# Narrower scores and shared-out probability blocks in the first batches, and permuted weight columns, in a fused attention and gated feed-forward kernel

## The chip, the cores and the metric

The kernel runs on one core of a Trainium2 chip. The metric is the device time of one execution in microseconds (us), the median of several runs. Inside the core, TensorE (PE in the profile) multiplies matrices, VectorE (DVE), ScalarE (ACT) and GpSimd (POOL) do the element work, and the queue of SyncE (SP) issues the transfers between device memory and the on-chip memory. PEld is the part of TensorE that loads the stationary operand of a multiplication. The engines run side by side, each through its own list of instructions in a fixed order, and wait for one another by semaphores.

## What is computed

Attention over 8 batches, 8 heads, 576 positions, 64 features for each head, and then two matrix products with a gate between them, over the 4608 rows that the attention gives.

```python
scores = q @ k.T / 8            # (8, 8, 576, 576)
rel = pos[:, None] - pos[None, :]
mask_local   = (rel >= 0) & (rel < 32)                      # heads 0 to 3
mask_strided = (rel >= 0) & (pos % 32 equal on both sides)  # heads 4 to 7
attn = softmax(where(mask, scores, -1e9)) @ v
x = attn as (4608, 512)
h = x @ w_in                    # (4608, 2048)
out = (h * clip(h + 3, 0, 6) / 6) @ w_out                   # (4608, 512)
```

So few scores count: a local head needs a band of 32 positions, a strided head 18 positions for each of the 32 residues.

## The kernel before

**The feed-forward part** carries nearly all of the multiplying. Every operand is held as a high and a low part, and a product is three matmuls (high by high, high by low, low by high), each 128 by 128 by 512 columns. Batches 0, 1 and 2 are done one by one in `ffn`: for each of 16 chunks `fc`, four first products over the four head pairs `c` (lines 848 to 850), a gate (ACT line 769, DVE line 772), a split of the gated tile into `gh` (ACT line 783) and `gl` (POOL line 787), and four second products into the accumulators `acc` (lines 825 to 827). Batches 3 to 7 and the leftover rows are done two at a time with a scheme that needs seven products for eight (Strassen's): `super_tile` and `fast_tile`, whose first products are lines 1121 to 1123 (tiles `P`) and whose second products in `fast_tile` are lines 1444 to 1446 (tiles `cP`). The last take the weights as the stationary operand and pick every second column of them, `d::2`, so that a later transpose on DVE gives rows of the output.

**The weights** are loaded once, in 32 parts of 128 by 512, during the first batch. `weight_part` sends each through a chain: two ACT passes (lines 281 and 285), a join on DVE (line 289), a rounded copy `hi` on ACT or POOL (lines 295 and 297), and the difference `lo` on POOL (line 301). The tiles are `rawi`/`rawo`, `fi`/`fo`, `wi`/`wo`.

**The attention** is done in pairs of heads (`pair`; c = 0 and 1 are local, 2 and 3 strided). For each pair and each of its two heads j: scores on PE into `ps`, a masked copy into the tile `e`, a maximum (DVE, line 637), its subtraction (POOL, line 641), the exponential (ACT, line 645), a sum and its inverse (DVE, lines 651 and 654), the scaling (POOL, line 658). Then the 32 by 32 blocks of `e` are transposed and set out into the mostly zero tiles `atloc` or `atstr`, and PE multiplies these with the values into `pv`. Two forms of these steps matter here.

- Scores of strided pairs are `wide` (64 rows by 36 columns, line 593) in every batch but 1: fewer matmuls, but half of the result is unused, so four ACT copies of 32 partitions (line 619) pick the rest out and a POOL instruction adds the mask (line 633). The narrow form (line 601) takes twice the matmuls and one DVE instruction (line 626) does copy and mask together.
- Blocks are set out by DVE in batches 0 and 1: a transpose for each block, 4 for a strided head (line 677), 6 for a local head (line 680). From batch 2 on one DVE transpose turns all blocks in place (line 683), and ACT copies them out (lines 690 and 693). The two local pairs of batch 0 do it by PE instead.

Finally `keep_x` takes `pv` into the operand of the first product, in two or three pieces: a rounded copy (ACT, line 419) and, in batches 0 and 1, the low part (DVE, line 422). The pieces of a pair share one key, so that copy, difference, copy, difference follow each other.

**The order of the work** is made when the program is built. Every step is handed to `Plan.op` with the engine or engines that may do it, a cost, what it reads and writes and a due time; `Plan.emit` sorts them into one list for each engine by a list schedule over these costs. Where it sees PE idle in the first 100 us it puts in matmuls on an identity tile (`idle`, line 1562) that feed nothing. `T0` is the planned time of the first batch's products, from which the other due times follow. No engine leaves its list's order at run time.

Of the kernel before, what the change touches and what calls it, by code (L numbers as in the profile page):

```python
# [29 lines left out]
TOK = 512  # L30
TURNS = ((0, 2, 1, 3), (2, 0, 3, 1)) + ((0, 2, 1, 3),) * 6
AHEAD = 27.0
OPEN = 6.0
HIENG = {"ACT": 0.63, "POOL": 0.7}

T0 = 44.0
TILE = 98.5
SUPER = 182.0  # L40
SECOND = 142.0
# [132 lines left out]
def attention_ffn(ctx: ExitStack, tc, q, k, v, w_in, w_out, out):  # L174
# [85 lines left out]
    def weight_part(k, w, g, i):  # L260
        key = wkey(w, g, i)
        fc = FQ * g if w == "i" else FQ * g + i + 1
        due = T0 + fc * TILE / NFC - 5.0 + 0.01 * k
        fkey = ("x", 1, 1 - (k // 2 % 2 if k < 20 else 0), k % 2)
        name = f"{w}{g}{i}"

        def load():
            if w == "i":
                src = w_in[i * P:(i + 1) * P, g * TOK:(g + 1) * TOK]
            else:  # L270
                src = w_out[(g * FQ + i) * P:(g * FQ + i + 1) * P, :]
            raw = new(wp, key, [P, TOK, 2], I32, f"raw{name}")
            nc.sync.dma_start(raw, src.bitcast(I32).rearrange("p (n t) -> p n t", t=2))

        def bits():
            raw = tiles[key]
            return raw.rearrange("p n t -> p (n t)")[:, :TOK]

        def high():
            f = new(xp, fkey, [P, TOK], I32, f"f{name}")  # L280
            nc.scalar.activation(f.bitcast(F32), tiles[key][:, :, 1].bitcast(F32), AF.Prelu, scale=2.0 ** -112, alpha=2.0 ** 32)

        def low():
            raw = tiles[key].bitcast(U16).rearrange("p n (t u) -> p n t u", u=2)[:, :, 0, 1]
            nc.scalar.activation(bits(), raw, AF.Copy, scale=2.0 ** -13, bias=2.0 ** -14 - 0.5)

        def join():
            f = tiles[fkey]
            nc.vector.scalar_tensor_tensor(out=f, in0=f, scalar=3, in1=bits(),  # L289
                                           op0=ALU.logical_shift_left, op1=ALU.bitwise_or)  # L290

        def hi(e):
            t = new(wp, key, [P, 2, TOK], F32R, f"w{name}")
            if e == "ACT":
                nc.scalar.copy(t[:, 0], tiles[fkey].bitcast(F32))
            else:
                nc.gpsimd.tensor_copy(t[:, 0], tiles[fkey].bitcast(F32))

        def lo():
            t = tiles[key]  # L300
            nc.gpsimd.tensor_tensor(out=t[:, 1], in0=tiles[fkey].bitcast(F32), in1=t[:, 0].bitcast(F32), op=ALU.subtract)  # L301
# [21 lines left out]
    def either(us):  # L323
        return {"POOL": us, "DVE": us}

    def zero(key, pool, shape, dtype, us, due, name):

        def go(e):
            on(e).memset(new(pool, key, shape, dtype, name), 0.0)
            if key[0] == "e":  # L330
                t = tiles[key]
                on(e).memset(t[:, :NQB * WIN].rearrange("p (u x) -> p u x", x=WIN)[:, :, 2 * PAD:], 1.0e-9)
                on(e).memset(t[:, NQB * WIN:NQB * WIN + 8 * PAD].rearrange("p (u x) -> p u x", x=PAD)[:, :, NPOS:NPOS + 1], 1.0e-9)
        op(either(us), 0, go, writes=[key], due=due)

    def timing(g):
        b = g // NPAIR
# [60 lines left out]
    def x_keys(b, c):  # L398
        return [("x", b, c, i) for i in range(2)] if b < 2 else [raw_key(b, c)]

    def keep_x(nm, b, c, puts, due):

        xk, lk = x_keys(b, c), ("left", c, b)
        strided = c >= NPAIR // 2
        begun = []
        for n, (bkey, what, place, size, rest) in enumerate(puts):
            def to(i, place=place, rest=rest):
                return place(left[c][:, LEFT * b:LEFT * b + LEFT] if rest else tiles[xk[i]])

            def homes():  # L410
                if not begun:
                    begun.append(1)
                    for i, x in enumerate(xk):
                        new(xp, x, [P, TOK], F32R if b < 2 else F32, f"x{nm}{i}")

            def hi(bkey=bkey, what=what, to=to, rest=rest):
                if not rest:
                    homes()
                nc.scalar.copy(to(0), what(tiles[bkey.key]))

            def lo(bkey=bkey, what=what, to=to):
# [4 lines left out]
            op("ACT", 0.15 + size * (0.0019 if strided else 0.00085), hi, reads=[bkey] + (xk if rest else []), writes=kk, give=bkey if last and whole else None, due=due + n)  # L426
            if not whole:
                op("DVE", 0.15 + size * (0.002 if strided else 0.00105), lo, reads=[bkey], writes=kk, give=bkey if last else None, due=due + 0.2 + n)

# [3 lines left out]
    def pair(g):  # L433
# [237 lines left out]
        for j in range(2):  # L671
            def turn(j=j):
                at, e = tiles[akeys[j]], e_whole(j)
                for a in range(n // PAD):
# [3 lines left out]
                        continue  # L678
                    for h in range(2):
                        nc.vector.transpose(at[PAD * (a + h):PAD * (a + h) + PAD, :, rows], e[rows, :, PAD * h:PAD * h + PAD])  # L680
            if b >= 2:
                def flip(j=j):
                    nc.vector.transpose(e_whole(j)[:, :, :2 * PAD if loc else PAD], e_whole(j)[:, :, :2 * PAD if loc else PAD])  # L683

# [10 lines left out]
                def again(j=j):  # L695
                    nc.gpsimd.memset(e_whole(j)[:, :, NPOS:NPOS + 1], 1.0e-9)
# [20 lines left out]
        def values():  # L717
# [12 lines left out]
        op("PE", 1.25 * slow, values, reads=[*akeys, *vkeys], writes=[*vb, *xk, lk], take=vb, due=due - 1001,  # L730
           room=0.0 if early else ROOM, mode="v")
        if first:
            half = S // 2
# [56 lines left out]

    def out_ops(i, uk, name, rows, due, last):
        def ob():
            o = new(xp, uk, [P, DM], F32, f"ob{name}_{i}")
            if last and i % 2:
                nc.vector.tensor_scalar_mul(o, tiles["acc", i], 1.0 / 6.0)
            else:
                nc.scalar.activation(o, tiles["acc", i], AF.Copy, scale=1.0 / 6.0)

        def store():
            o = tiles[uk]  # L800
# [9 lines left out]
    def ffn(b):  # L810
        s0, puts = start[b], []
        chunk = TILE / NFC
        xk = {c: x_keys(b, c) if b < 2 else [("x", 1, c, i) for i in range(2)] for c in range(NCC)}

        def mm2(fc, gk):
            wkeys = [wkey("o", fc // FQ, fc % FQ), wkey("o", fc // FQ, fc % FQ) + ("lo",)]
# [17 lines left out]
        def first_product(fc):  # L834
# [3 lines left out]
            for n_, c in enumerate(TURNS[b]):  # L838
                wkeys = [wkey("i", fc // FQ, c), wkey("i", fc // FQ, c) + ("lo",)]

                def mm1(n_=n_, c=c, wkeys=wkeys):
# [9 lines left out]
                op("PE", 0.683, mm1, reads=xk[c] + wkeys, writes=[pk],  # L851
                   due=s0 + (fc + n_ * 0.12) * chunk, mode="f")
            return fc, pk, uk, gk

# [430 lines left out]
    def fast_tile(si):  # L1285
# [87 lines left out]
        def second_of(s):  # L1373
# [5 lines left out]
            for j, nm in enumerate(SECONDS):  # L1379
# [53 lines left out]
                for d in range(2):  # L1433
                    bank = ("acc", d + 2 * (nm in ("P2", "P5", "P3")))

                    def mm(d=d, bank=bank, gks=gks, wk=wk, fresh=fresh, nm=nm):
# [3 lines left out]
                        w = home(wk).rearrange("p q (h d) -> p q h d", h=2)  # L1440
                        for q in range(2):
                            gh, gl = (half_of(gks[q], x) for x in range(2))
                            wh, wl = (w[:, q, h, d::2] for h in range(2))
                            nc.tensor.matmul(acc, wh, gh, start=fresh and q == 0, stop=False, skip_group_check=not fresh)  # L1444
                            nc.tensor.matmul(acc, wh, gl, start=False, stop=False, skip_group_check=not fresh)  # L1445
                            nc.tensor.matmul(acc, wl, gh, start=False, stop=q == 1, skip_group_check=not fresh)  # L1446
# [62 lines left out]
    def first_tiles():  # L1509
        tiles["qplain"] = ap.tile([P, S + STRIDE * PAD], F32, tag="qq", name="qplain")  # L1510
        tiles["kplain"] = ap.tile([P, PAD + 2 * S], F32, tag="kk", name="kplain")
        nc.gpsimd.memset(tiles["kplain"][:, :PAD], 0.0)
        nc.gpsimd.memset(tiles["qplain"][:, S:].rearrange("c (r m) -> c r m", m=PAD)[:, :, NPOS:], 0.0)
        tiles["at64"] = ap.tile([P, 2, 3 * QB], F32, tag="vt", name="at64")
    op("POOL", 0.1, first_tiles, writes=["plain", ("at64", 0), ("at64", 1)], due=-30)
# [80 lines left out]
```

## Time and profile before

| | |
|---|---|
| median of 3 runs | 875.98 us (873.19 to 877.65) |
| profiled execution | 873.75 us, of which the profile's span is 871.9 us |
| PE busy | 851.9 us, 98% of the span |
| DVE, ACT, POOL busy | 539.3, 557.8, 614.7 us (62, 64, 70%) |
| mean granted TensorE clock | 0.992 |

All rows are of that one profiled execution; the profiled execution is 2.2 us under the median. A busy PE is not always PE at its full pace, since matmuls overlap: the pace is read from the starts of neighbouring matmuls. The rows of a group give the count, the busy time in us and the mean of one in ns; a row of the timeline gives the start and the duration in us and, in brackets, the idle time of the engine before it and what ended it.

### The profile page before, as it was taken

What the parts mean: (1) busy time and instruction counts of PE and PEld (TensorE: products, weight loads), DVE (VectorE), ACT (ScalarE), POOL (GpSimd) and SP (SyncE); (2) the same over time, 40 slices, a digit from 0 to 9 for tenths busy, and PEclk for the clock granted to TensorE, in tenths of its full rate; (3) what the DMA queues carried; (4) which work ended last, traced back from release to release, by engine and by line L of the source; (5) the groups of instructions that cost most, each with busy time, mean ns of one, the idle gap of its engine ahead of it and who ended that gap; (6) DMA issues with size and microseconds to landing.
All of it is one profiled execution on the core that took longest, in us unless ns stands there. A gap on an engine that the chain in (4) does not pass through costs nothing.

```text
span 871.9 us, 18946 instructions
## 1 busy us (share of the span) xinstructions
PE 851.9 (98%) x6962; PEld 687.7 (79%) x6962; DVE 539.3 (62%) x898; ACT 557.8 (64%) x1246; POOL 614.7 (70%) x606
## 2 busy tenths in 40 slices
PE   9889999999999999999999999999999999999996
PEld 6667778878878788888888888788888778888884
DVE  5698877344544548454546672566776987655586
ACT  3697657678778766777668855776645555454441
POOL 4688876688447799756767993666974978667572
PEclk9899999999999999999999999999999999999998
DMA  8968714888974456899999998976566577766536
GB/s 214 322 140 243 220 28 93 236 265 239 299 200 111 112 141 163 233 250 259 259 262 282 300 284 213 253 188 198 181 195 183 178 207 214 231 190 188 178 121 145
DMA packets 323308, 179.12 MB, mean 205 GB/s; under 512 B 182864, under 2 KB 300368, under 8 KB 323216
## 3 DMA queue, kind: packets, MB, share of 16 engines
q1 hardware_dynamic: 318564, 176.27, 71.9%
q10 hardware_dynamic: 4652, 1.64, 0.9%
q8 instruction: 55, 0.90, 0.4%
q14 instruction: 37, 0.30, 0.1%
HBM read 136.97 MB, written 40.89 MB: 204 GB/s over the span
## 4 chain that ended last, share of the span: by engine, by line
PE 87%; DMA 5%; POOL 3%; DVE 2%; issue 1%; ACT 1%; SPq 0%; ACTq 0%; POOLq 0%
PE P L1121 9%; PE P L1123 8%; PE P L1122 8%; PE cP L1444 6%; PE cP L1446 6%; PE cP L1445 6%; PE acc L825 5%; PE ph L848 5%; PE acc L827 5%; PE acc L826 4%; PE ph L850 4%; PE ph L849 4%; PE acc L1206 4%; PE acc L1208 3%; PE acc L1207 3%; PE pv L392 2%
## 5 line engine op out<-in xcount | busy, mean ns | idle before, releaser
L1462 DVE SCALAR_TENSOR_TENSOR C<-cP,C 128x512 f32<-128x512 f32 x96 | 65.7, 688 | 44.9 <-PE cP L1446 44.3
L787 POOL TENSOR_TENSOR gl<-u,gh 128x512 fp32r<-128x512 f32 x48 | 65.2, 1359 | 32.2 <-ACT gh L783 16.0
L1133 DVE TENSOR_TENSOR G<-P,G 128x512 f32<-128x512 f32 x64 | 44.0, 689 | 65.6 <-PE P L1123 52.8
L1121 PE MATMUL P<-B_T,wr 128*128 128x512 f32 x192 | 76.2, 397 | 3.4 <-ACT G L1128 2.3
L825 PE MATMUL acc<-wo,gh 128*128 128x512 f32 x192 | 77.2, 402 | 0.0
L827 PE MATMUL acc<-wo,gl 128*128 128x512 f32 x192 | 75.2, 392 | 0.1
L1123 PE MATMUL P<-B_T,wr 128*128 128x512 f32 x192 | 75.0, 391 | 0.0
L1122 PE MATMUL P<-B_T,wr 128*128 128x512 f32 x192 | 74.9, 390 | 0.0
L826 PE MATMUL acc<-wo,gh 128*128 128x512 f32 x192 | 74.9, 390 | 0.0
L1128 ACT COPY G<-P 128x512 f32<-128x512 f32 x64 | 37.6, 587 | 54.1 <-PE P L1123 53.8
L1359 POOL TENSOR_TENSOR sp<-G,sp 128x512 fp32r<-128x512 f32 x34 | 47.2, 1399 | 25.6 <-ACT sp L1355 23.4
L658 POOL TENSOR_TENSOR e<-e,st 128x144 f32<-128x144 f32 (+1 forms) x64 | 44.6, 700 | 20.2 <-DVE st L654 17.2
L772 DVE SCALAR_TENSOR_TENSOR u<-u,ph 128x512 f32<-128x512 f32 x48 | 32.7, 684 | 37.9 <-ACT u L769 37.8
L848 PE MATMUL ph<-x,wi 128*128 128x512 f32 x128 | 51.9, 406 | 2.0 <-DVE u L772 1.1
L693 ACT COPY atloc<-e 32x192 f32<-32x192 f32 x144 | 50.8, 353 | 2.5 <-DVE e L683 1.1
L849 PE MATMUL ph<-x,wi 128*128 128x512 f32 x128 | 50.1, 391 | 1.1 <-DVE fo L289 0.7
L769 ACT ACTIVATE u<-ph,three 128x512 f32<-128x512 f32 x48 | 33.0, 688 | 27.7 <-PE ph L850 27.3
L850 PE MATMUL ph<-x,wi 128*128 128x512 f32 x128 | 50.2, 392 | 0.5 <-POOL wi L301 0.5
L1121 PE MATMUL P<-B_B,wr 128*128 128x512 f32 x120 | 47.1, 393 | 0.0
L637 DVE TENSOR_REDUCE st<-e 128x8 f32<-128x144 f32 (+1 forms) x64 | 25.6, 413 | 34.5 <-POOL e L633 34.3
L1123 PE MATMUL P<-B_B,wr 128*128 128x512 f32 x120 | 46.8, 390 | 0.0
L1122 PE MATMUL P<-B_B,wr 128*128 128x512 f32 x120 | 46.8, 390 | 0.0
(604 smaller groups left out, 2669.1 us busy)
## 6 DMA issues: line engine op xcount, KB each, us to landing
wr<-dA SPq DMA_DIRECT2D x72, 256.0 KB
or<-do SPq DMA_DIRECT2D x32, 512.0 KB
wr<-dSu SPq DMA_DIRECT2D x48, 256.0 KB
wr<-dSv SPq DMA_DIRECT2D x48, 256.0 KB
or<-do SPq DMA_DIRECT2D x48, 256.0 KB
rawi<-in_moe_w_in_dram SPq DMA_DIRECT2D x16, 512.0 KB
rawo<-in_moe_w_out_dram SPq DMA_DIRECT2D x16, 512.0 KB
do<-wo SPq DMA_DIRECT2D x16, 512.0 KB
```

The lines of the kernel that those rows point to most:

```text
L787: (nc.vector if tail else nc.gpsimd).tensor_tensor(out=to, in0=src(), in1=tiles[gk[0]].bitcast(F32), op=ALU.subtract)
L825: nc.tensor.matmul(acc, gh, woh, start=fc == 0, stop=False)
L826: nc.tensor.matmul(acc, gh, wol, start=False, stop=False)
L827: nc.tensor.matmul(acc, gl, woh, start=False, stop=end)
L848: nc.tensor.matmul(ph, wih, xh, start=n_ == 0, stop=False)
L849: nc.tensor.matmul(ph, wih, xl, start=False, stop=False)
L850: nc.tensor.matmul(ph, wil, xh, start=False, stop=n_ == NCC - 1)
L1121: nc.tensor.matmul(ph, wh, xh, start=fresh and k == 0, stop=False, skip_group_check=not fresh)
L1122: nc.tensor.matmul(ph, wh, xl, start=False, stop=False, skip_group_check=not fresh)
L1123: nc.tensor.matmul(ph, wl, xh, start=False, stop=k == 1, skip_group_check=not fresh)
L1444: nc.tensor.matmul(acc, wh, gh, start=fresh and q == 0, stop=False, skip_group_check=not fresh)
L1462: nc.vector.scalar_tensor_tensor(out=tiles[ck], in0=tiles[bank], scalar=1.0 / 6.0, in1=tiles[ck], op0=ALU.mult, op1=ALU.add)
```

## The change

Three things are changed.

1. **Strided pairs of batch 0** take the narrow scores of batch 1, and the strided pairs of batch 0 and all pairs of batch 1 turn their blocks by one transpose in place. In batches 0 to 4 (`b < FREE`) the copies that set the blocks out are planned one by one, each on ACT, POOL or DVE, where it was DVE alone (batches 0 and 1) or ACT alone (from batch 2).
2. **`keep_x`** has a key for each piece in batches 0 and 1, so that the copy of the second piece no longer waits for the difference of the first; copies of leftover rows get a due time 3 us later. `T0` goes from 44 to 42.
3. **Columns of `w_out`** are stored so that within each half of 256 the even ones stand ahead of the odd ones. The second products of `fast_tile` then read 128 neighbouring columns. The rounded copy and the difference of each `w_out` part read with a step of two, and `out_ops`, which takes `acc` to the output tile `ob`, writes with a step of two.

```diff
-T0 = 44.0
+T0 = 42.0
...
+        def whole():
+            f = tiles[fkey].bitcast(F32)
+            return f if w == "i" else f.rearrange("p (h e d) -> p h d e", h=2, d=2)
+
+        def part(x):
+            t = tiles[key][:, x]
+            return t if w == "i" else t.rearrange("p (h d e) -> p h d e", h=2, d=2)
...
-                nc.gpsimd.tensor_copy(t[:, 0], tiles[fkey].bitcast(F32))
+                nc.gpsimd.tensor_copy(part(0), whole())
...
-            nc.gpsimd.tensor_tensor(out=t[:, 1], in0=tiles[fkey].bitcast(F32), in1=t[:, 0].bitcast(F32), op=ALU.subtract)
+            nc.gpsimd.tensor_tensor(out=part(1), in0=whole(), in1=part(0).bitcast(F32), op=ALU.subtract)
...
-            kk = [lk] if rest else xk
+            kk = [lk] if rest else xk if whole else [("xh", b, c, n)] + ([] if n else xk)
...
-                op("DVE", ..., lo, reads=[bkey], writes=kk, ..., due=due + 0.2 + n)
+                op("DVE", ..., lo, reads=[bkey, ("xh", b, c, n)], writes=[("xl", b, c, n)], ..., due=due + 0.2 + n)
...
-        wide = not loc and b != 1
+        wide = not loc and b > 1
...
-            if b >= 2:
+            if b >= 2 or b == 1 or b == 0 and not loc:
...
-                op("ACT", 6 * 0.31 if loc else 4 * 0.36, spread, reads=[ekeys[j]], writes=[akeys[j]], due=due - 1.9 + j)
+                if b < FREE:
+                    for a in range(n // PAD):
+                        for h in range(1 + loc):
+                            def set_out(e, a=a, h=h, j=j):
...
+                                if e == "ACT":
+                                    nc.scalar.copy(at, x)
+                                else:
+                                    on(e).tensor_copy(at, x)
...
+                            op({"ACT": 0.33, "POOL": 0.42, "DVE": 0.37} if loc else {"ACT": 0.4, "POOL": 0.5, "DVE": 0.44}, 0, set_out,
+                               reads=[ekeys[j], ("zero",) + akeys[j]], writes=own, due=due - 1.9 + j)
+                else:
+                    op("ACT", 6 * 0.31 if loc else 4 * 0.36, spread, reads=[ekeys[j]], writes=[akeys[j]], due=due - 1.9 + j)
...
-            o = new(xp, uk, [P, DM], F32, f"ob{name}_{i}")
+            o = new(xp, uk, [P, DM], F32, f"ob{name}_{i}").rearrange("p (h e d) -> p h d e", h=2, d=2)
+            acc = tiles["acc", i].rearrange("p (h d e) -> p h d e", h=2, d=2)
...
-                            wh, wl = (w[:, q, h, d::2] for h in range(2))
+                            wh, wl = (w[:, q, h, P * d:P * d + P] for h in range(2))
```

Counted over the whole program: DVE loses 56 transposes of single blocks and gains 12 in place and 62 copies; ACT loses 47 copies of blocks, the 16 copies of wide scores and 6 rounded weight copies; POOL gains 41 copies of blocks, 6 rounded weight copies and 8 small fills and loses 4 mask additions. PE gets 64 score matmuls more and 5 identity matmuls less (each of these runs as two passes). The transfers are the same, in nearly the same order.

In what follows the number behind a tile's name tells two tiles apart (`e_130` and `e_228` are the two heads of a pair; `st` holds maxima and sums; `ps_20` is the scores of pair c = 2, head 0; `pe` is the PE's turned block of the local pairs).

On ACT, at the strided pair c = 2 of batch 0 (rows of before, then of the changed kernel), the exponentials of the local pair's two heads stood apart:

```order
L645 ACTIVATE e_130<-e_130 96x6x64
L619 COPY e_130<-ps_20_450 32x8x18 x4
L645 ACTIVATE e_228<-e_228 96x6x64
L619 COPY e_228<-ps_21_451 32x8x18 x4
L506 COPY kt_3_289<-kp_30_530 128x288
```

```order
L654 ACTIVATE e_186<-e_186 96x6x64
L654 ACTIVATE e_233<-e_233 96x6x64
L515 COPY qt_3_289<-qp_30_524 128x288
L515 COPY qt_3_289<-qp_31_525 128x288
L654 ACTIVATE e_186<-e_186 128x8x18
```

The eight copies of wide scores are gone, and the second exponential follows the first.

On DVE, a little later, where the turn of pair 2 and the first steps of the local pair c = 1 meet (before, then changed):

```order
L677 STREAM_TRANSPOSE atstr_269<-e_130 32x8x32 x4
L651 TENSOR_REDUCE st_2_508<-e_228 128x8
L626 TENSOR_TENSOR e_130<-ps_10_599,mband 96x6x64
L628 MEMSET e_130 32x32
L654 RECIPROCAL st_2_508<-st_2_508 128x8
L637 TENSOR_REDUCE st_1_677<-e_130 96x6
L626 TENSOR_TENSOR e_228<-ps_11_600,mband 96x6x64
L628 MEMSET e_228 32x32
L677 STREAM_TRANSPOSE atstr_272<-e_228 32x8x32 x4
L422 TENSOR_TENSOR x_01_703<-pv_00_638,x_00_702 128x288
L651 TENSOR_REDUCE st_1_677<-e_130 96x6
L637 TENSOR_REDUCE st_1_677<-e_228 96x6
```

```order
L692 STREAM_TRANSPOSE e_186<-e_186 128x256
L517 COPY kt_3_290<-kp_31_580 128x288
L660 TENSOR_REDUCE st_2_545<-e_233 128x8
L663 RECIPROCAL st_2_545<-st_2_545 128x8
L692 STREAM_TRANSPOSE e_233<-e_233 128x256
L635 TENSOR_TENSOR e_186<-ps_10_626,mband 96x6x64
L637 MEMSET e_186 32x32
L635 TENSOR_TENSOR e_233<-ps_11_627,mband 96x6x64
L637 MEMSET e_233 32x32
L646 TENSOR_REDUCE st_1_707<-e_186 96x6
L646 TENSOR_REDUCE st_1_707<-e_233 96x6
```

Between the first mask addition of pair 1 and the maximum of its second head there stood a turn of four transposes, a low part and a sum; now the two heads' steps follow each other.

On POOL, around the scaling of pair 3 (before, then changed):

```order
L301 TENSOR_TENSOR wi_840<-fi_727,wi_840 128x512
L1529 MEMSET vloc 32x128
L658 TENSOR_TENSOR e_130<-e_130,st_3_785 128x8x18
L658 TENSOR_TENSOR e_228<-e_228,st_3_785 128x8x18
L301 TENSOR_TENSOR wi_917<-fi_828,wi_917 128x512
L301 TENSOR_TENSOR wo_924<-fo_902,wo_924 128x512
```

```order
L667 TENSOR_TENSOR e_233<-e_233,st_3_841 128x8x18
L718 COPY atstr_270<-e_186 32x8x32 x2
L307 CAST wi_965<-fi_900 128x512
L705 MEMSET e_186 128x8
L718 COPY atstr_273<-e_233 32x8x32
L310 TENSOR_TENSOR wi_948<-fi_858,wi_948 128x512
L705 MEMSET e_233 128x8
L310 TENSOR_TENSOR wi_965<-fi_900,wi_965 128x512
```

Three of the eight block copies of pair 3 stand on POOL, ahead of weight parts.

More of the change, by code (lines that the diff above doesn't have):

```diff
@@ L32 @@
 AHEAD = 27.0
+LEFTS = 3.0
+FREE = 5
 OPEN = 6.0
 HIENG = {"ACT": 0.63, "POOL": 0.7}
-T0 = 44.0
+T0 = 42.0
 TILE = 98.5
@@ L290, in join @@
                                            op0=ALU.logical_shift_left, op1=ALU.bitwise_or)
+        def whole():
[4 more added lines that the diff above has]
+            return t if w == "i" else t.rearrange("p (h d e) -> p h d e", h=2, d=2)
         def hi(e):
-            t = new(wp, key, [P, 2, TOK], F32R, f"w{name}")
+            new(wp, key, [P, 2, TOK], F32R, f"w{name}")
             if e == "ACT":
-                nc.scalar.copy(t[:, 0], tiles[fkey].bitcast(F32))
+                nc.scalar.copy(part(0), whole())
             else:
-                nc.gpsimd.tensor_copy(t[:, 0], tiles[fkey].bitcast(F32))
+                nc.gpsimd.tensor_copy(part(0), whole())
         def lo():
-            t = tiles[key]
-            nc.gpsimd.tensor_tensor(out=t[:, 1], in0=tiles[fkey].bitcast(F32), in1=t[:, 0].bitcast(F32), op=ALU.subtract)
+            nc.gpsimd.tensor_tensor(out=part(1), in0=whole(), in1=part(0).bitcast(F32), op=ALU.subtract)
         op("SP", 0.53, load, writes=[key], due=-49 + 0.01 * k if k < 4 else -48.4 + 0.01 * k if k < 6 else -2 + 0.1 * k if k < 16 else due - 20.0, early=7.0 if k < 16 else due - 30.0, after=1.6 if k < 16 else 1.25)
@@ L333, in go @@
                 on(e).memset(t[:, NQB * WIN:NQB * WIN + 8 * PAD].rearrange("p (u x) -> p u x", x=PAD)[:, :, NPOS:NPOS + 1], 1.0e-9)
-        op(either(us), 0, go, writes=[key], due=due)
+        op(either(us), 0, go, writes=[key, ("zero",) + key], due=due)
     def timing(g):
@@ L422, in lo @@
                 nc.vector.tensor_tensor(out=to(1), in0=what(tiles[bkey.key]), in1=to(0).bitcast(F32), op=ALU.subtract)
-            kk = [lk] if rest else xk
             last = all(x[0] is not bkey for x in puts[n + 1:])
             whole = rest or b >= 2
-            op("ACT", 0.15 + size * (0.0019 if strided else 0.00085), hi, reads=[bkey] + (xk if rest else []), writes=kk, give=bkey if last and whole else None, due=due + n)
+            kk = [lk] if rest else xk if whole else [("xh", b, c, n)] + ([] if n else xk)
+            op("ACT", 0.15 + size * (0.0019 if strided else 0.00085), hi, reads=[bkey] + (xk if n or rest else []), writes=kk, give=bkey if last and whole else None, due=due + n + LEFTS * rest)
             if not whole:
-                op("DVE", 0.15 + size * (0.002 if strided else 0.00105), lo, reads=[bkey], writes=kk, give=bkey if last else None, due=due + 0.2 + n)
+                op("DVE", 0.15 + size * (0.002 if strided else 0.00105), lo, reads=[bkey, ("xh", b, c, n)], writes=[("xl", b, c, n)], give=bkey if last else None, due=due + 0.2 + n)
     def pair(g):
@@ L729, in values @@
                                      ats[j][:, i].rearrange("p (a m) -> p a m", a=4)[:, :, :NPOS], start=True, stop=True)
-        op("PE", 1.25 * slow, values, reads=[*akeys, *vkeys], writes=[*vb, *xk, lk], take=vb, due=due - 1001,
+        op("PE", 1.25 * slow, values, reads=[*akeys, *vkeys] + [(x, i) for x in akeys for i in range(8) if b < FREE], writes=[*vb, *xk, lk], take=vb, due=due - 1001,
            room=0.0 if early else ROOM, mode="v")
@@ L792, in ob @@
         def ob():
-            o = new(xp, uk, [P, DM], F32, f"ob{name}_{i}")
+            o = new(xp, uk, [P, DM], F32, f"ob{name}_{i}").rearrange("p (h e d) -> p h d e", h=2, d=2)
+            acc = tiles["acc", i].rearrange("p (h d e) -> p h d e", h=2, d=2)
             if last and i % 2:
-                nc.vector.tensor_scalar_mul(o, tiles["acc", i], 1.0 / 6.0)
+                nc.vector.tensor_scalar_mul(o, acc, 1.0 / 6.0)
             else:
-                nc.scalar.activation(o, tiles["acc", i], AF.Copy, scale=1.0 / 6.0)
+                nc.scalar.activation(o, acc, AF.Copy, scale=1.0 / 6.0)
         def store():
@@ L813, in ffn @@
         xk = {c: x_keys(b, c) if b < 2 else [("x", 1, c, i) for i in range(2)] for c in range(NCC)}
+        parts = {c: [(x, b, c, n) for x in ("xh", "xl") for n in range(3)] if b < 2 else [] for c in range(NCC)}
         def mm2(fc, gk):
@@ L850, in mm1 @@
                     nc.tensor.matmul(ph, wil, xh, start=False, stop=n_ == NCC - 1)
-                op("PE", 0.683, mm1, reads=xk[c] + wkeys, writes=[pk],
+                op("PE", 0.683, mm1, reads=xk[c] + parts[c] + wkeys, writes=[pk],
                    due=s0 + (fc + n_ * 0.12) * chunk, mode="f")
@@ L1512, in first_tiles @@
         nc.gpsimd.memset(tiles["kplain"][:, :PAD], 0.0)
+        nc.gpsimd.memset(tiles["qplain"][:, 2 * S:2 * S + SPARE], 0.0)
         nc.gpsimd.memset(tiles["qplain"][:, S:].rearrange("c (r m) -> c r m", m=PAD)[:, :, NPOS:], 0.0)
```

5 lines of the change are left out of this document (added).

## Prediction

> **What bounds the kernel now.** I read first the engines' shares, then the work of each engine by stretches, then the starts of neighbouring matmuls, and last the timeline of the first 60 us.
>
> ```profile
> PE 851.9 (98%) x6962; PEld 687.7 (79%) x6962; DVE 539.3 (62%) x898; ACT 557.8 (64%) x1246; POOL 614.7 (70%) x606
> ```
>
> TensorE is busy for 98% of the span, so only two things shorten the program: matmuls that follow each other faster, or less waiting of TensorE. The stretches tell where each is to be had (columns: stretch, length, then PE, PEld, DVE, ACT, POOL busy us, granted clock, DMA share, GB/s).
>
> ```profile
> 56.00:140.00 84.00, 82.33 (x829) 64.61 (x832) 69.12 (x129) 56.71 (x103) 70.51 (x65) 1.00 0.56 145
> 180.00:240.00 60.00, 60.00 (x633) 48.50 (x630) 26.61 (x58) 48.20 (x134) 39.70 (x50) 1.00 0.89 267
> 740.00:840.00 100.00, 100.00 (x434) 82.30 (x433) 58.42 (x81) 45.07 (x74) 63.99 (x48) 1.00 0.61 185
> 24.00:32.00 8.00, 6.95 (x166) 5.78 (x166) 5.86 (x17) 4.57 (x10) 1.70 (x4) 0.62 0.82 222
> 33.13:57.56 24.43, 22.07 (x282) 15.97 (x280) 17.74 (x37) 20.45 (x48) 21.97 (x23) 1.00 0.86 259
> ```
>
> From 180 us on TensorE never stops (60.00 of 60, 100.00 of 100): there the other engines' work is covered and only the pace counts. In the first product stage (56 to 140) 1.7 us of waiting are left. Ahead of it lies the head, where the attention of batch 0 decides when the second products can begin. A busy TensorE there is partly filler and score work, so its 22.07 of 24.43 does not make it the bound; POOL with 21.97 of 24.43 is as near.
>
> **The weight columns.** Here the starts decide, twelve matmuls of the one kind and 26 of the other, each run without a gap.
>
> ```profile
> 609.38 0.39 PE L1121 MATMUL P<-B_B,wr 128*128 128x512 f32 x1
> ...
> 611.87 0.39 PE L1123 MATMUL P<-B_B,wr 128*128 128x512 f32 x1
> ...
> 842.29 0.39 PE L1444 MATMUL cP<-B_B,or 128*128 128x512 f32 x1
> ...
> 848.12 0.39 PE L1445 MATMUL cP<-sp,or 128*128 128x512 f32 x1
> ```
>
> First products take (611.87 - 609.38) / 11 = 226.4 ns each, second products of the fast tiles (848.12 - 842.29) / 25 = 233.2 ns. Shapes and clock are the same, and B_B appears as an operand of both kinds; what differs is the weights' step of two. The weight loads differ by as much:
>
> ```profile
> L1122 PEld LDWEIGHTS P<-B_T,wr 128*128 128x128 f32 x192 | 36.1, 188 | 7.5
> L1444 PEld LDWEIGHTS cP<-sp,or 128*128 128x128 f32 x88 | 17.1, 194 | 3.7 <-DVE C L1462 0.2
> ```
>
> 194 against 188 ns, 6 ns. The groups of L1444 hold 224 matmuls, and L1445 and L1446 as many, 672 in all. By the load groups the gain is 672 x 6 = 4.0 us, by the starts 672 x 6.8 = 4.6 us. I take 4.2 us, near the groups, which average over far more instructions than the starts. The lower bound is 0, if the step is not the cause. Nothing covers this time: it is TensorE's own. The following drain by DVE (L1462, off TensorE's end in that stretch: 58.42 of 100) keeps up.
>
> [...]
>
> **The step moves elsewhere.** The rounded copies and differences of `w_out` now read with a step, `ob` writes with one. The nearest row is a strided ACT write in the head (three times wider step) beside its plain twin, with `ob` itself:
>
> ```profile
> 10.04 0.67 ACT L506 COPY qplain<-qp 128x288 f32<-128x288 f32 x1 [6.87 <-PE qp L364]
> 12.04 0.40 ACT L506 COPY qplain<-qp 128x288 f32<-128x288 f32 x1 [0.34 <-PE qp L364]
> L797 ACT ACTIVATE ob<-acc 128x512 f32<-128x512 f32 x12 | 6.7, 596 | 1.3 <-PE acc L827 1.2
> ```
>
> 0.27 us more for 288 columns is at most 0.5 us for 512. The 20 `ob` lie at five ends of product stages: at worst 5 x 0.5 = 2.5 us, if TensorE waited for each; it is at 60.00 of 60 while ACT has 48.20, so I take 0. The cover would be gone if the next stage needed an accumulator at once.
>
> **The head.** The rows, in order of time:
>
> ```profile
> 15.80 1.61 POOL L641 TENSOR_TENSOR e<-e,st 96x384 f32<-96x384 f32 x2 [8.41 <-DVE st L637]
> 19.16 1.12 ACT L619 COPY e<-ps 32x144 f32<-32x144 f32 x4 [1.12 <-PE ps L593]
> 20.31 0.53 ACT L645 ACTIVATE e<-e 96x384 f32<-96x384 f32 x1
> 24.48 1.79 DVE L677 STREAM_TRANSPOSE atstr<-e 32x256 f32<-32x256 f32 x4 [0.65 <-POOL e L658]
> 25.05 1.43 PE L364 MATMUL pe<-ident,e 96*64 96x96 f32 x19 [2.37 <-issue]
> 28.00 0.56 DVE L626 TENSOR_TENSOR e<-ps,mband 96x384 f32<-96x384 f32 x1 [1.24 <-PE ps L601]
> 29.82 0.09 DVE L628 MEMSET e<- 32x32 f32 x1
> 29.83 1.75 DVE L677 STREAM_TRANSPOSE atstr<-e 32x256 f32<-32x256 f32 x4
> 32.45 0.54 DVE L637 TENSOR_REDUCE st<-e 96x6 f32<-96x384 f32 x1
> 33.13 1.50 POOL L641 TENSOR_TENSOR e<-e,st 96x384 f32<-96x384 f32 x1 [2.88 <-DVE st L637]
> 57.56 3.02 POOL L787 TENSOR_TENSOR gl<-u,gh 128x512 fp32r<-128x512 f32 x2
> 58.71 0.40 PE L825 MATMUL acc<-wo,gh 128*128 128x512 f32 x1
> ```
>
> *Exponential.* POOL had both heads of pair 0 ready at 15.80 + 1.61 = 17.41, but the second exponential stood on ACT behind four copies that waited until 19.16 for wide scores. ACT had been free since 18.04. The copies are gone, so it can run 20.31 - 18.04 = 2.3 us earlier. It feeds the turned block at 25.05, ahead of which TensorE stood for 2.37 us. That idle time is put down to issue, not to a wait, so I take half, 1.1 us.
>
> *Turns.* On DVE, the first mask addition of pair 1 begins at 28.00 and the second head's maximum ends at 32.99, for which POOL's subtraction waits 2.88 us. The order now leaves 0.56 + 0.09 + 0.55 + 0.09 for additions and fills and 0.55 + 0.54 for the two maxima: 2.4 us instead of 5.0, so 2.6 us earlier; the turn, the low part and the sum between them go ahead or behind. What is late next is POOL's list.
>
> *POOL to its first gl.* Durations:
>
> ```profile
> L633 POOL TENSOR_TENSOR e<-e,mtri 128x144 f32<-128x144 f32 x28 | 13.9, 499 | 23.5 <-ACT e L619 23.5
> L301 POOL TENSOR_TENSOR wo<-fo,wo 128x512 fp32r<-128x512 f32 x16 | 21.3, 1338 | 0.7 <-ACT wo L295 0.4
> L297 POOL CAST wi<-fi 128x512 fp32r<-128x512 f32 x8 | 5.3, 668 | 3.2 <-DVE fi L289 3.2
> L297 POOL CAST wo<-fo 128x512 fp32r<-128x512 f32 x6 | 4.5, 750 | 1.8 <-DVE fo L289 1.8
> L1149 POOL TENSOR_TENSOR sp<-sp 128x256 f32<-128x256 f32 x32 | 24.5, 766 | 1.1
> L696 POOL MEMSET e<- 128x8 f32 x24 | 2.7, 114 | 14.0 <-ACT atstr L690 10.0 <-DVE kplain L526 4.0
> ```
>
> From 33.13 on two masks go (1.0 us), two weight differences go behind it (2.7), two rounded copies come (1.4), small fills add 0.2, and three block copies come. A block copy on POOL isn't in the trace: it lies between a fill (0.11) and a two-operand instruction of as many columns (0.77). A weight copy of twice the columns takes 0.67 to 0.75, half of that 0.33 to 0.38, so I take 0.40: 1.2 us. Sum: -1.0 - 2.7 + 1.4 + 0.2 + 1.2 = -0.9 us.
>
> The last two follow each other on POOL: the first `gl` comes 2.6 + 0.9 = 3.5 us earlier. But TensorE fills that time with first products, some six of which (1.4 us by their pace) then stand behind it, so 2.1 us of it count. With the exponential the head gives 1.1 + 2.1 = 3.2 us. The bounds: all of it goes through, 2.3 + 2.6 + 0.9 and, since the granted clock in 24 to 32 was 0.62 (3 us of full pace lost) and part of that could go with the gap, some 1.2 more, 7 us; or POOL's copies take 0.77 and the turns free nothing, +1.
>
> *At nothing:* 64 more score matmuls and five fillers less run where TensorE waits for other engines anyway. ACT loses eight copies of wide scores and four weight casts behind 26 us and gains three block copies there, so it is relieved. The in-place turn replaces four transposes of 0.44 by one (groups below), off the path. The new keys of `keep_x` save a few tenths that the sum of the turns holds already. The transfers and their queues stay.
>
> **The first product stage.** Between the first and the last `gl` of batch 0 POOL takes eight block copies (3.2), five rounded copies (3.5) and the two deferred differences (2.7): 9.4 us more. 70.51 + 9.4 = 79.9 of 84 still fit, with 4 us left. I take 0. DVE (69.12 of 84) takes 16 copies of about 0.4 and drops its transposes:
>
> ```profile
> L677 DVE STREAM_TRANSPOSE atstr<-e 32x256 f32<-32x256 f32 x32 | 13.9, 435 | 2.3 <-POOL e L658 1.9
> L683 DVE STREAM_TRANSPOSE e<-e 128x256 f32<-128x256 f32 x24 | 10.4, 439 | 9.2 <-POOL e L658 9.2
> ```
>
> Batches 2 to 4 move copies from ACT where TensorE has no gap: 0.
>
> **The sum.** 873.75 (the profiled execution) - 4.2 - 3.2 = 866.35. That execution is 2.2 us under the median, so 868.6 us against 875.98.
>
> **The rivals.**
>
> - *The step costs nothing.* The 6 ns belong to the other operand or to the result's place, and stay. Against it: loads and starts agree, and the second products read B_B too, as the first do. Only the head is left: 875.98 - 3.2 = 872.8. Chance 0.10. [...]
> - *The head gives nothing.* POOL's own rate, 21.97 of 24.43, sets the first `gl`, and its list comes out as long as before (a block copy of 0.67 would do it); or weight loads by DMA (share 0.86) come no earlier. 875.98 - 4.2 = 871.8. Chance 0.15.
> - *The head gives all.* The gap at 25.05 goes, the clock stays up: 875.98 - 4.2 - 7 = 864.8. Chance 0.12.
> - *POOL becomes the bound of the first product stage.* A block copy stands in POOL's list behind the turn it reads; if it comes before its turn, every `gl` behind it waits. Copies at 0.77 give 6.2 instead of 3.2, so 82.9 of 84; eight waits for one DVE instruction and a turn (0.69 + 0.57, estimates from DVE's share and rows) add 10. From 84 on it decides; 8.9 us over, with no gain in the head: 875.98 - 4.2 + 8.9 = 880.7. Against it speak the room of 4 us by the nearer prices and that the turn has DVE's idle 15 us to run in. Chance 0.06. [...]
>
> **How the numbers follow.** The forecast has the other 0.57. A difference under 0.5%, 4.4 us, can hardly be told from none, so "faster" means under 871.6. That takes in the forecast nearly whole and the third rival: 0.68. The first two rivals (just above the line) and an edge of the forecast are the same: 0.27. The last is slower, mostly: 0.05. The range runs from 863.5 (the third rival and a microsecond below it) to 874.5 (the first and 1.6 for the head's upper bound and `ob`); it leaves out the last rival and an edge of the third, about 0.12.
>
> **What would show it.** Weight loads of the fast tiles' second products at 188 ns and starts 227 ns apart; the second exponential near 18.1; POOL's subtraction of pair 1 near 30.5; the first `gl` near 54; POOL under 80 in the first stage, and no more than 2 us of TensorE's waiting in it. I am wrong if the loads stay at 194, if POOL's block copies take over 0.7, or if TensorE waits for `gl` or `xl` after 60 us.

## The result and the profile after

The changed kernel is slower: a median of 884.12 us (882.82 to 887.19, 6 runs) against 875.63 us (873.19 to 877.65, 6 runs), a ratio of 1.0112 with a 95% interval of 1.0095 to 1.013. The profiled execution took 886.62 us, its span is 884.7 us. The forecast was 868.6 us.

The page's line of the engines after:

```profile
PE 850.3 (96%) x7080; PEld 687.1 (78%) x7080; DVE 572.1 (65%) x921; ACT 535.5 (61%) x1178; POOL 630.8 (71%) x656
```

TensorE is busy for 96% of the span instead of 98%. The stretches say where (columns: stretch, length, then PE, PEld, DVE, ACT, POOL busy us, granted clock, DMA share, GB/s); first the kernel before, then the changed one:

```profile
24.00:58.00 34.00, 30.49 (x450) 22.67 (x450) 25.17 (x55) 26.44 (x61) 24.11 (x28) 0.90 0.84 249
0.00:60.00 60.00, 53.00 (x934) 40.14 (x935) 41.17 (x94) 37.45 (x84) 37.02 (x61) 0.94 0.83 232
```

```profile
56.00:140.00 84.00, 80.40 (x816) 63.70 (x813) 63.63 (x103) 60.88 (x116) 74.40 (x77) 0.98 0.51 138
24.00:58.00 34.00, 24.08 (x506) 19.38 (x507) 15.07 (x41) 18.27 (x44) 16.82 (x29) 0.65 0.77 242
0.00:60.00 60.00, 44.94 (x1011) 35.88 (x1012) 28.71 (x77) 25.72 (x58) 28.93 (x63) 0.77 0.80 232
```

In the first 60 us TensorE works 8.1 us less, at a granted clock of 0.77 instead of 0.94, although it issues more matmuls (1011 against 934). The other engines work less too. What TensorE waits for there, picked from the list of its waits (total, times, longest), before and after:

```profile
PE pe L364 <- issue: 2.4, 1, 2.4
PE ps L593 <- issue: 0.8, 1, 0.8
```

```profile
PE ps L610 <- issue: 4.2, 1, 4.2
PE qp L373 <- issue: 3.8, 1, 3.8
PE pv L753 <- issue: 2.9, 1, 2.9
PE pv L753 <- ACT atstr L716: 2.8, 2, 1.8
```

The three long ones, 10.9 us together, are put down to "issue": no semaphore, no engine. In the timeline they stand in the middle of runs of small matmuls, not at a step's beginning:

```profile
22.22 1.71 PE L373 MATMUL qp<-ident,qn 72*64 72x72 f32 x24 [3.78 <-issue]
36.96 0.62 PE L753 MATMUL pv<-atstr,v 128*64 128x72 f32 x5 [2.87 <-issue]
43.16 0.30 PE L610 MATMUL ps<-kt,qt 64*32 64x18 f32 x5 [4.24 <-issue]
```

The last five of a group of 128 score matmuls came 4.24 us after the others. The page's rows on the transfers name a queue that carries instructions, before and after:

```profile
q8 instruction: 55, 0.90, 0.4%
```

```profile
q8 instruction: 56, 0.92, 0.4%
```

These are 55 and 56 packets of 16,384 bytes. TensorE has 13,924 and 14,160 instructions in the two profiles (matmuls and weight loads), about 253 for each packet. The records of that queue, set beside TensorE's stops, give this table (us; "count" is the number of TensorE's matmuls and weight loads that had begun):

```
kernel          TensorE stops at count   from    to      packet of the queue   resumes after its end by
before               951                22.68  25.05     22.63 to 23.56        1.49
changed              953                18.44  22.22     20.01 to 20.96        1.26
changed             1458                34.09  36.96     34.66 to 35.53        1.43
changed             1714                38.92  43.16     40.87 to 41.81        1.34
```

The stops of the changed kernel lie 505 and 256 instructions apart. With the semaphore instructions that stand among TensorE's records counted in, the four stops fall at 961, 961, 1473 and 1729, that is 512 and 256 apart. TensorE goes on 1.3 to 1.5 us after a packet has landed. I read this as a TensorE that had run out of instructions; e9 tries that reading. The narrow scores show 64 matmuls more in the trace for a pair, and with each its weight load: 256 instructions more in the head for the two pairs. As work they are almost free: 2.98 us of busy time for both pairs, against 2.64 for the wide ones. As instructions they are not, by this reading: ahead of the first stop of the changed kernel TensorE used up the 250 or so behind count 699 in 1.6 us (16.8 to 18.4), where the kernel before took 4.6 (18.1 to 22.7), and the next packet did not begin until 20.01.

How late the work then is, read from the starts of the 3216 large matmuls (tiles ph, acc, P, cP): the start of the n-th in the kernel before, and how much later it starts in the others.

```
n-th large matmul         1     60    200    384   1152   1500   2544   3216
before               39.0   59.9   98.6  146.7  354.2  445.0  707.0  863.1
changed              +5.3   +9.4  +10.8  +13.5  +14.7  +14.7  +15.9  +13.1
e1 columns           +0.6   +1.5   +1.9   +1.9   +1.9   +1.9   +1.0   -1.7
e9 scores twice     +10.9  +10.8  +11.0  +11.1  +11.1  +11.1  +10.6   +7.8
e3 wide scores back  -3.8   +1.8   +6.7   +6.1  +13.4  +14.7  +12.1   +9.4
e13 T0 = 42          -3.2   -0.5   -0.4   -0.4   +1.8   +3.1   -0.8   -3.6
e15 other cost       +1.4   +2.8   +3.7   +8.4   +9.5  +11.0   +8.1   +5.4
```

The changed kernel loses 9.4 us up to the 60th (to 70 us), 5.3 more up to the 1500th (460 us), and wins back some 3 at the end, where the permuted columns act.

### The profile page after: what moved, and what is told of

It is laid out like the page before. It is cut to its first block, busy times and chain, and to the rows that moved or that the text cites. A ratio compares the mean times of both kernels' runs of the same rounds, so it can differ in the third digit from the quotient of the medians.

```text
span 884.7 us, 19228 instructions
## 1 busy us (share of the span) xinstructions
PE 850.3 (96%) x7080; PEld 687.1 (78%) x7080; DVE 572.1 (65%) x921; ACT 535.5 (61%) x1178; POOL 630.8 (71%) x656
## 4 chain that ended last, share of the span: by engine, by line
PE 80%; POOL 6%; DVE 4%; issue 4%; DMA 3%; ACT 2%; SPq 0%; POOLq 0%; ACTq 0%; DVEq 0%
PE P L1148 8%; PE P L1149 8%; PE P L1150 8%; PE cP L1471 5%; PE cP L1473 5%; PE cP L1472 5%; PE ph L875 5%; PE ph L876 4%; PE acc L852 4%; PE ph L877 4%; PE acc L854 4%; PE acc L853 4%; PE acc L1233 2%; PE acc L1235 2%; PE acc L1234 2%
## 5 line engine op out<-in xcount | busy, mean ns | idle before, releaser
L667 POOL TENSOR_TENSOR e<-e,st 96x384 f32<-96x384 f32 (+1 forms) x64 | 43.9, 689 | 29.6 <-DVE st L663 29.3
L1155 ACT COPY G<-P 128x512 f32<-128x512 f32 x64 | 37.6, 587 | 43.7 <-PE P L1150 43.0
L660 DVE TENSOR_REDUCE st<-e 96x6 f32<-96x390 f32 (+1 forms) x64 | 27.4, 428 | 49.0 <-ACT e L654 26.6
L875 PE MATMUL ph<-x,wi 128*128 128x512 f32 x128 | 53.6, 419 | 1.8 <-DVE u L797 1.8
L876 PE MATMUL ph<-x,wi 128*128 128x512 f32 x128 | 50.9, 398 | 0.6 <-issue 0.6
L877 PE MATMUL ph<-x,wi 128*128 128x512 f32 x128 | 50.9, 398 | 0.6 <-POOL wi L310 0.6
L1148 PEld LDWEIGHTS P<-B_T,wr 128*128 128x128 f32 x192 | 36.0, 188 | 13.9 <-ACT G L1155 3.9
L692 DVE STREAM_TRANSPOSE e<-e 128x256 f32<-128x256 f32 (+1 forms) x60 | 29.9, 501 | 25.8 <-POOL e L667 23.0
```

The source lines that it names most:

```text
L1148: nc.tensor.matmul(ph, wh, xh, start=fresh and k == 0, stop=False, skip_group_check=not fresh)
```

## The experiments

Each is compared with runs of the kernel before on the same chip (medians 874.2 to 874.9 us). The theories: **A**, instruction supply: the narrow scores' many instructions come too late in the head. **B**: the block copies on three engines bring new waits. **C**: the new keys and due times of `keep_x` and `T0` do. **D**: any new order of the lists loses, whatever the edit.

**e1, the columns alone.** Every engine's order stays that of before.

```diff
-wh, wl = (w[:, q, h, d::2] for h in range(2))
+wh, wl = (w[:, q, h, P * d:P * d + P] for h in range(2))
```

(with `part`, `whole` and the output side as in the change)

> Only the permuted columns of w_out (rounded copy, difference, ob and the reads of the second products); every engine's order is that of before. Theory: the step's price was real, since the excess of the fast tiles' matmuls over 227 ns fell by 4.9 us between the two traces; so 875.6 - 4.5 = 871 us (869.5 to 872.5). Rival (the step costs nothing and the shorter steps after the change came from waits elsewhere): 875 to 876.

870.93 us, ratio 0.9954 (0.9932 to 0.9976), that is 4.0 us (2.1 to 6.0) won. Weight loads of the kernel e1, second products of the fast tiles:

```profile
L1454 PEld LDWEIGHTS cP<-sp,or 128*128 128x128 f32 x88 | 16.5, 188 | 3.5
```

188 ns instead of 194: the step cost what the rows said.

**e2 to e4, the parts of the change against each other.** e2 is before with narrow scores alone (`wide = not loc and b > 1`, and the small fill they need); e3 the changed kernel with `wide = not loc and b != 1`; e4 the changed kernel with `if b >= 2:` at the turns and `FREE = 0`.

> Before, with narrow scores for the strided pairs of batch 0 alone. Theory A (instruction supply: TensorE's instructions come in blocks of 256 by DMA, late while the other transfers are dense, and the narrow form has twice as many): idle time put down to issue in the first 60 us grows from 3.2 to 8 or more, granted clock halves for longer, time 881 to 886 us. Theory B (the block copies on three engines do the harm): 874 to 877, issue time as before.

> The changed kernel with wide scores in batch 0 again, all else kept. Theory A: issue time in the head falls from 10.9 to 3 to 5 us, the time to 868 to 873. Theory B: 881 to 885, issue time may fall but waits for block copies stay.

> The changed kernel with the blocks set out as before (turns by DVE in batches 0 and 1, ACT from 2 on), narrow scores and permuted columns kept. Theory A: issue time in the head stays at 8 to 11 us, time 878 to 884; what it gains on 884 is the later waits (about 3 us between 140 and 500). Theory B: 870 to 873.

e2: 894.96 us, ratio 1.0227 (1.0197 to 1.0256), more than theory A gave (7.3 us of stops in the head and one more of 1.9 at 118 us, which ended 1.4 us after a packet; 4.4 us of waiting for parts of `wi` and 3.0 for the gate in the new order). e3: 883.25, ratio 1.0094 (1.0069 to 1.012). e4: 884.57, ratio 1.0111 (1.0081 to 1.014). The stops at counts 953 and 1714 are there in e2 and e4 as in the changed kernel, and gone in e3 (one at 951, 1.65 us, as before). So the stops belong to the narrow scores. But e3 wins only a microsecond, and its time is the one that theory B gave: without the narrow scores the kernel is still 12 us slower than the columns alone (e1), and without the block copies (e4) it is 14 slower. The loss is there with either part left out. Theory A explains the head and not the total. In the timeline of e3 TensorE waits for block copies and for the gate (last row: DVE ahead of the gate of 78.17):

```profile
32.91 1.21 PE L753 MATMUL pv<-atstr,v 128*64 128x72 f32 x30 [0.74 <-POOL atstr L718]
50.95 1.70 PE L753 MATMUL pv<-atstr,v 128*64 128x72 f32 x30 [2.71 <-POOL atstr L718]
78.17 0.50 PE L875 MATMUL ph<-x,wi 128*128 128x512 f32 x1 [1.25 <-DVE u L797]
92.94 0.50 PE L875 MATMUL ph<-x,wi 128*128 128x512 f32 x1 [1.18 <-DVE u L797]
135.13 0.50 PE L875 MATMUL ph<-x,wi 128*128 128x512 f32 x1 [1.58 <-DVE u L797]
74.60 2.79 DVE L718 COPY atstr<-e 32x256 f32<-32x256 f32 x3
```

ACT's part of the gate of 78.17 was done at 75.39; DVE's part began at 77.43, behind three block copies of 0.9 us each. So here the copies on DVE held up the gate. The gate of 135.13 has three copies (2.39 us) a few instructions ahead of it; that of 92.94 stands behind two joins of weight parts, 5.60 us.

**e9, the instructions alone.** e1 with each wide score matmul of batch 0 issued twice; no other engine's list changes.

```diff
-for i in range(2 * nblk):
+for i in [i for i in range(2 * nblk) for _ in range(2 if b == 0 else 1)]:
```

> Permuted columns only, with each wide score matmul of batch 0 issued twice in a row (the second writes the same result): as many TensorE instructions as the narrow form has, at the same places, while every other engine's list and the ACT copies and POOL masks stay. Theory A: its own work is about 2 x 0.6 us; the waits put down to issue grow from 1.8 to 5 to 11 us and the granted clock is halved longer, time 876 to 884 against 870.9. If the narrow form does its harm through the new order instead: 871 to 872.5.

881.28 us, ratio 1.005 (1.0019 to 1.008). Eight of the ten runs took 880 to 882 us, two 871.0 and 873.8, for which there is no trace. The timeline of TensorE in the profiled run (881.59):

```profile
18.18 2.06 PE L600 MATMUL ps<-kplain,qplain 64*64 64x36 f32 x119 [1.22 <-issue]
24.27 0.99 PE L371 MATMUL qp<-ident,qn 72*64 72x72 f32 x24 [3.63 <-issue]
38.89 0.98 PE L735 MATMUL pv<-atstr,v 128*64 128x72 f32 x11 [1.66 <-issue]
44.81 0.43 PE L600 MATMUL ps<-kt,qt 64*64 64x36 f32 x11 [1.96 <-issue]
```

8.5 us of stops at the counts 698, 953, 1459 and 1715, against 1.8 in e1, and the first large matmul comes 10.3 us later than in e1. The same counts stop other work here (values, not scores, at 1459), and the lag is constant from there on. This is shown, then: as many instructions as the narrow scores bring cost some 10 us in the head with nothing else changed, in most runs. Not all of it is supply: 6.6 us are stops, and 3.4 are the doubled matmuls' own time (5.96 us busy against 2.52, a part of it at a granted clock of 0.5), of which the narrow form has 0.3.

**e7 and e8, where the boundaries fall.** e1 with 23 warm-up matmuls of 64 columns, or 92 of 16, instead of 46 of 32.

```diff
-FEW = 46
+FEW = 23   # e8: 92
```

> Permuted columns only, with the 46 warm-up matmuls of 32 columns at the start replaced by 23 of 64: 92 TensorE instructions less ahead of the head, about the same warm-up time, every order kept. Theory A: the 256-instruction boundaries fall 92 instructions later in the program, so the 1.8 us of issue time near 24 us shrink to under 1, and the time by 0 to 1.5 us from 870.9. If instructions are not what TensorE waits for there, the 1.8 us stay where they are.

> Permuted columns only, with 92 warm-up matmuls of 16 columns instead of 46 of 32: 184 TensorE instructions more, nothing else moved. Theory A: boundaries come 184 instructions earlier, the waits put down to issue grow from 1.8 to 4 to 9 us, the granted clock is halved longer, time 873 to 879. If instructions don't matter: 871, issue time 1.8.

875.68 us, ratio 1.0001 (0.9973 to 1.003), and 876.46, ratio 1.0016 (0.9981 to 1.0051); their runs scatter over 9.9 and 12.7 us, and neither differs clearly from the kernel before. The issue rows of the waits, e7 and then e8:

```profile
PE ps L608 <- issue: 2.8, 1, 2.8
PE pv L735 <- issue: 0.9, 1, 0.9
```

```profile
PE idle L1570 <- issue: 4.1, 1, 4.1
PE ps L608 <- issue: 2.3, 1, 2.3
```

e8 did as expected (6.4 us). e7 did in part: the stop at count 951 is gone, but there are stops at 445 and 1203 in its place, and its median is no lower than that of e1. Its first packet landed at 14.39 us instead of 10.04 in e1, and TensorE came to count 191 at 9.9 us in e7 and at 4.9 in e1. In all 18 traces of this case the first seven packets began 0.3 to 9.3 us after TensorE had passed the counts 191, 445, 699, 951, 1205, 1459 and 1714, one packet for each count, and never before. Later packets, counted on in the same steps, began up to 3.0 us before their count in the kernel before and up to 4.7 in the changed one. What starts a packet is not shown.

**e5, e6, e10 to e12, the other parts.** e5: columns, keys, later leftovers and `T0 = 42` (hunks for scores and blocks left out, `FREE = 0`). e6: before with the blocks of batches 0 to 4 alone. e10 and e11: columns, and the blocks of batch 0 or of batches 1 to 4. e12: columns, keys and leftovers, `T0 = 44`.

> The changed kernel without its scores and its blocks: permuted columns, the keys of keep_x, the later leftovers and T0 = 42 are left. Theory A (narrow scores starve TensorE of instructions) and theory B (cut block copies bring new waits) both expect about the time of the columns alone, 871 us (868 to 873). Theory C (the new due times and keys already make an order that loses in the first product stages): 876 to 882, with waits of the first products for DVE's gate or POOL's gl.

> Before, with the blocks of batches 0 to 4 turned in place and copied one by one by ACT, POOL or DVE; wide scores, old columns, keys and T0. Theory B: 880 to 887, as the changed kernel with wide scores (883.25) without the 4 us of the columns; the waits name the block copies, the gate and gl. Theory A alone: 874 to 877. Theory C: 874 to 877 too.

> Permuted columns, and the blocks of batch 0's strided pairs turned in place and copied one by one by ACT, POOL or DVE; all later batches as before. Theory B with the harm in the head: 874 to 879. With the harm in the later batches: 869 to 873.

> Permuted columns, and the blocks of batches 1 to 4 copied one by one by ACT, POOL or DVE; batch 0 as before. Theory B with the harm in the first product stages: 874 to 880, with TensorE waiting for gl, the gate and block copies between 60 and 350 us; with the harm in the head: 869 to 873.

> Permuted columns and the keys of keep_x with the later leftovers, T0 = 44 as before; scores and blocks as before. If the keys themselves help: 867 to 870; if any new order loses some microseconds in the first product stages: 872 to 877 as with T0 = 42 (873.4).

```
e5 keys, T0 = 42     873.37 us   ratio 0.9994 (0.9975 to 1.0013)
e6 blocks 0 to 4     883.59      1.0102 (1.0076 to 1.0128)
e10 blocks 0         874.74      0.9995 (0.9976 to 1.0014)
e11 blocks 1 to 4    881.35      1.0063 (1.0045 to 1.008)
e12 keys, T0 = 44    879.20      1.0052 (1.0033 to 1.0071)
```

All are above the columns alone (870.93; e6 has the old columns, so some 4 us of its loss are theirs). That looked like a price of each part. But each also made the scheduler write all lists anew.

**e13 to e15, a new order and almost nothing else.** e1 with `T0 = 42`, with `T0 = 43`, or with the exponential planned 0.05 us longer (`0.25 + ...` for `0.2 + ...`): the work stays, but by their place in the traces some 1400 to 2900 of TensorE's 6962 matmuls differ, a few element instructions pass to another engine, and e15 has one identity matmul more. **e16** gives the changed kernel a new order in the same way (`T0 = 44`).

> Permuted columns only, with T0 = 42: the same instructions in a new order. If the order of before is a lucky or sought-out one and any new order loses (theory D): 874 to 881, as with the block copies. If block copies and keys do the harm themselves: 869 to 873.

> Permuted columns only, with T0 = 43. Theory D: 874 to 881. Otherwise 869 to 873.

> Permuted columns only, with the exponential planned 0.05 us longer: no instruction of the work changes, the order does. Theory D: 874 to 881. Otherwise 869 to 873.

> The changed kernel with T0 = 44. Narrow scores remain, so TensorE still waits for instructions in the head (8 to 11 us of issue time): 880 to 890 by theory A, whatever the order. Below 876 would speak against theory A.

e13: 870.67 us, ratio 0.9957 (0.9942 to 0.9973). e14: 874.23, 0.9998 (0.9976 to 1.0019). e15: 879.02, 1.0058 (1.0032 to 1.0084). Theory D is refuted as it was put, since e13 loses nothing. But a new order alone costs between nothing and 8 us. The first waits of TensorE in e15:

```profile
PE ph L856 <- DVE u L779: 3.4, 3, 2.6
PE pe L371 <- issue: 2.4, 1, 2.4
PE acc L835 <- POOL gl L794: 2.2, 3, 1.0
```

They are of the kind that e3 shows. So e5, e10 and e12 prove no price of keys or blocks; e11 lies 2 us beyond e15 by the medians and less than 1 by the ratios, which three orders can't settle. e3 lies 3 to 4 us beyond e15: none of the three orders loses as much. e16: 887.97 us, ratio 1.0162 (1.0121 to 1.0203), with stops at the same counts 953, 1458 and 1714, 12.3 us in all: this other order does not heal the narrow scores. e1 and e13 are the two versions that beat both kernels.

## Why the prediction was wrong

- **The weight columns: right.** Forecast 4.2 us, measured 4.0 (2.1 to 6.0), by the cause that was named: the second products now start 227 ns apart like the first, and the rows read:

```profile
L1149 PEld LDWEIGHTS P<-B_T,wr 128*128 128x128 f32 x192 | 36.1, 188 | 7.2
L1471 PEld LDWEIGHTS cP<-sp,or 128*128 128x128 f32 x88 | 16.5, 188 | 3.5
```

 The rival that the step costs nothing is refuted.
- **"At nothing: 64 more score matmuls": this step failed.** I priced them as work that TensorE has idle time for, and as work they do cost only 0.3 us. They cost by their number: the stops in the head grow from 3.2 us to 10.9, and the first large matmul comes 5.3 us later; in e9, where only the number changes, the stops grow by 6.6. The row that should have warned me was quoted: 2.37 us "issue" ahead of the turned blocks. I halved it as a doubtful wait for the exponential. In fact TensorE stood at count 951 until 1.49 us after a packet of instructions, and every other trace with the same warm-up stops at 951 or 953 too.
- **The shorter chains happened and brought nothing.** Both exponentials of pair 0 run as one, and the additions and maxima of pair 1 take 2.2 us (forecast 2.4), in the changed kernel's timeline:

```profile
17.36 0.94 ACT L654 ACTIVATE e<-e 96x384 f32<-96x384 f32 x2
31.44 0.56 DVE L635 TENSOR_TENSOR e<-ps,mband 96x384 f32<-96x384 f32 x1 [0.45 <-PE ps L610]
32.66 0.97 DVE L646 TENSOR_REDUCE st<-e 96x6 f32<-96x384 f32 x2
33.32 1.60 POOL L650 TENSOR_TENSOR e<-e,st 96x384 f32<-96x384 f32 x1 [1.25 <-DVE st L646]
65.38 2.85 POOL L812 TENSOR_TENSOR gl<-u,gh 128x512 fp32r<-128x512 f32 x2
```

 But the chain begins 3.4 us later (31.44 against 28.00), since its scores wait behind the first stop; the first `gl` comes at 65.38, not near 54. So the head's term of the sum, 3.2 us, failed as well. It is not there even without the narrow scores: e3 is 3.8 us ahead at the first large matmul and 1.8 behind at the 60th.
- **The first product stage: too kind.** From the first to the last `gl` of batch 0 (before, then after; columns as above):

```profile
57.56:144.19 86.63, 85.31 (x886) 67.44 (x887) 70.74 (x133) 58.22 (x107) 73.14 (x67) 1.00 0.56 147
65.38:160.15 94.77, 90.13 (x906) 70.89 (x905) 73.60 (x125) 67.35 (x134) 83.25 (x86) 1.00 0.51 134
```

 POOL takes 10.1 us more, near the 9.4 of the forecast, and in the whole stage TensorE waits only 0.4 us for `gl`: that POOL became the bound, as the last rival said, is not borne out. Yet the term was not nothing. TensorE stood 3.6 us from 60 to 140 (limit named: 2) and 3.1 from 140 to 500, a stretch in which it had no gap before. I had taken it that work which fits the busy shares costs nothing in the planned order. e13 to e15 show that another order of the same work can lose up to 8 us. How much of the 5.3 us is the copies' own stays open. (That TensorE never stops from 180 us on was read too widely, too: before the change it is busy for 360.00 us of the 360 from 140 on, but for 236.64 of the 240 from 500 on.)
- **Block copies: right on POOL, wrong on DVE.** Groups of the changed kernel, and the spread of the DVE copies (minimum, median, maximum in ns):

```profile
L718 POOL COPY atloc<-e 32x192 f32<-32x192 f32 x24 | 9.6, 402 | 9.7 <-DVE e L692 7.2 <-DVE st L663 0.8 <-PE pv L401 0.7
L718 POOL COPY atstr<-e 32x256 f32<-32x256 f32 x17 | 7.0, 413 | 2.9 <-DVE e L692 2.2
L718 DVE COPY atloc<-e 32x192 f32<-32x192 f32 x34 | 26.6, 781 | 0.8
L718 DVE COPY atstr<-e 32x256 f32<-32x256 f32 x28 | 17.1, 610 | 0.9
```

```profile
L718 DVE COPY atloc<-e x34: 250/387/2651, 103.8 to 319.0; 32x192 f32<-32x192 f32 x34
L718 DVE COPY atstr<-e x28: 283/439/1311, 54.7 to 334.5; 32x256 f32<-32x256 f32 x28
```

 POOL takes the 0.40 us of the forecast in the mean. DVE takes 43.7 us for its 62 copies, where 0.4 each made 25.

Of the rivals none named what happened. The forecast had no case in which TensorE runs short of instructions; its chance for slower rested on POOL alone. What is shown is that the stops come with the narrow scores and cost time in the head. What is not shown is a full account of the 8.5 us: with the narrow scores taken out (e3) the kernel is hardly faster, and there the share of the order and the share of the block copies stay open.

## What to carry to other kernels

Idle time put down to "issue" on TensorE was not spare time here: each of the three long stops of the changed kernel, 10.9 us together, ended 1.3 to 1.4 us after a packet of the instruction queue. So count the instructions between such stops, and look for that queue's packets. Where many small matmuls follow each other in a few microseconds, weigh a form with half as many instructions against a shorter chain on the other engines: in e9 the score matmuls of batch 0 issued twice, with nothing else changed, made the first large matmul 10.3 us later. And where a scheduler rewrites the lists after every edit, time a few orders of the same work (e13 to e15: 870.7 to 879.0 us) before a few microseconds are given to the edit.

## What the hardware showed that was not expected

- TensorE's stops in the head fell on the same instruction counts, whatever stood there: every kernel with the same warm-up stopped at 951 to 953, and some also at 699, at 1205, at 1458 or 1459, or at 1711 to 1715; with other warm-ups e7 stopped at 445 and 1203 and e8 at 701 and 1461. Neighbouring counts are 252 to 256 apart. Counted with the semaphore instructions among TensorE's records, the stops fall at 705, 961 and 1729 in the kernel before and at 961, 1473, 1729 and 2497 (0.65 us, at 85.8 us) in the changed one: whole multiples of 256 apart, without exception. TensorE went on 1.2 to 1.8 us after a packet of 16,384 bytes had landed; the packets that ended these stops took 0.9 to 1.6 us. Two small waits put down to "issue" (0.2 us in e3, 0.7 in e15) follow no packet. The long stops of the changed kernel fell in its first 60 us, at a DMA share of 0.80. That dense transfers make the packets late, as theory A supposes, was not tried by an experiment; from 180 to 240 us, at a share of 0.89, TensorE of the kernel before was busy for 60.00 of 60 us, with 4.5 to 19.1 us for every 256 instructions instead of the 1.4 us ahead of the changed kernel's first stop.
- A copy on DVE took 0.25 to 0.29 us in the 7 cases where POOL was working for less than half of it, and 0.76 us in the mean of the other 55, up to 2.65. POOL's own copies took 0.40 to 0.41 in the mean, 0.80 at most. Why a copy on DVE took longer beside POOL's work is not shown.
